# Two GEMM layers of a mixture of experts on one core: the gates' broadcast load and half a layer-two product are moved in the instruction order

## The chip, the cores and the metric

The kernel runs on one core of a Trainium2 chip. The metric is device time in microseconds (us): the median of three executions, 2082.51 us (2081.88 to 2083.3).

## The reference, cut to what matters

Attention and a first MoE come first; the change touches the second MoE alone:

```python
# x: 2304 tokens x 512; w1: 8 experts x 512 x 1024; w2: 8 x 1024 x 512; P: gates, 2304 x 8
P = np.exp(logits - logits.max())
for _ in range(8):
    P /= P.sum(1, keepdims=True) + 1e-09
    P /= P.sum(0, keepdims=True) + 1e-09
    P *= N / E
for e in range(E):
    h = np.maximum(x @ w1[e], 0.0)      # layer one
    out += P[:, e:e+1] * (h @ w2[e])    # layer two
```

## The kernel before, in words

The second MoE runs over three blocks of 768 tokens, and in each block over 16 *quads*, two per expert; a quad m is 512 of an expert's 1024 hidden columns. m counts on over the blocks: m = 0 to 15 is block 0 (its own code, which also prepares the weights and writes them to DRAM), 16 to 31 block 1, 32 to 47 block 2.

Layer one of a quad is 14 products (two 2x2 block multiplications of seven products each, as `GP` lists them). Layer two is 14 half products (seven, as `YP` lists them, each for two halves of the output columns). Float32 is kept by splitting each operand into a high and a low part, so every product or half product is six TensorE matmuls of 384 columns. Layer one's results `rb` (PSUM) are joined and rectified by VectorE and ScalarE into tiles `R`; each `R` is multiplied with the gates (`scaled`, line 1476), and sums and high/low splits of it (lines 1481 to 1500) are layer two's operands `rb`, `rt`. Layer two's results `y` are added to accumulators `a` by VectorE (line 1536).

`scaled` needs the gates of one expert and one token block on all 128 partitions: tile `pb`, 128 x 768 floats, filled by `load_pb` (line 1461) with one DMA that reads six rows of 128 floats for every partition. One `pb` serves two quads, and there are two buffers. Weights come by DMA too: `load_w1` (line 818) brings one layer-one operand `w1o` (256 KB), always the one that is used eight products after the product that has just been written down, into the buffer that this product freed (eight buffers). `w2_op` (line 1512) brings one layer-two operand `w2o` (512 KB; used by two half products) for the next quad; there are nine buffers. Every DMA of this part is issued by SP, in the order in which the code stands, on one queue.

The engines run their instructions in the order in which this code is written; nothing reorders them. Two kinds of code write it:

- `step(m, s)`, 14 steps a quad, for the quads at the ends of a block: m = 16, 17, 31, 32, 33, 47. A step has product s of quad m and then half product s of quad m - 1. In m = 16 there is no such half; steps 0 to 5 hold the last `values` of block 0 instead, whose sums go to `out` by DMA (line 1317), and after step 6 the memory pool of block 0 is closed and its space is given to the tiles of the later blocks, `w2o` among them.
- `run_quad(m)` for quads 18 to 30 and 34 to 46 (`in_runs`): first a *product run*, the quad's 14 products one after the other (in the order `RUN_STEPS`; 14 in that list stands for product 0 of the next quad), then a *layer-two run*, the 14 half products of quad m - 1. The first quad of such a stretch (18, 34) is the *entry*, the last one (30, 46) *leaves*: its product run has no product of the next quad, so only 13 products in that list.

`load_pb` for the next expert stands in every odd quad: in `step` at s == 4, in `run_quad` after product 4 of the product run. The `w2_op` of a quad stand at odd steps; in `run_quad` they are in the layer-two run.

Of the kernel before, what the change touches and what calls it, by code (L numbers as in the profile page):

```python
# [25 lines left out]
def raw(ap):  # L26

    return ap.bitcast(F32)
# [3 lines left out]
def attention_moe_moe2(  # L32
# [40 lines left out]
    NQ = NP // 2  # L73
    PER = NPF // 2
    STEPS = 14
# [50 lines left out]
    def mm3(ps, lhs, rhs, first, last, **kw):  # L126
        (lh, ll), (rh, rl) = lhs, rhs
        nc.tensor.matmul(ps, lhsT=lh, rhs=rh, start=first, stop=False, **kw)  # L128
        nc.tensor.matmul(ps, lhsT=lh, rhs=rl, start=False, stop=False, **kw)  # L129
        nc.tensor.matmul(ps, lhsT=ll, rhs=rh, start=False, stop=last, **kw)  # L130
# [581 lines left out]
    Y_RUN = [YP[i] for i in (0, 1, 4, 2, 5, 3, 6)]  # L712
# [77 lines left out]
    def in_runs(m):  # L790

        return NQ <= m < NB * NQ - 1 and 2 <= m % NQ < NQ - 1
# [398 lines left out]
    def g_product(n, p):  # L1191
        o, b, bk = GP[p]
        first = p in (0, 1, 3)
        if first:
            gb[bk] = g_bank(f"g{bk}") if n else y_bank(f"g{bk}")
        w, x = slab[n][:, o] if n < NP else w1q.pop(7 * n + p), xop[b]
        for k in range(2):
            mm3(
                gb[bk][:, :HALF], (w[:, k, 0], w[:, k, 1]), (x[:, 0, k], x[:, 1, k]), first and k == 0, k == 1,
                skip_group_check=True,  # L1200
            )
# [254 lines left out]
    def load_pb(blk, e):  # L1456

        pbs[blk, e] = pp.tile([P, 2 * HALF], F32, name="pb", tag="pb", bufs=2)
        nt = 2 * HALF // P
        src = d_p.rearrange("(t e) p -> e t p", e=E)[e, blk * nt : (blk + 1) * nt]  # L1460
        nc.sync.dma_start(
            pbs[blk, e].rearrange("p (t c) -> p t c", t=nt), src.unsqueeze(0).to_broadcast([P, nt, P])
        )
# [3 lines left out]
    total = NB * NQ  # L1467
# [4 lines left out]
    def scaled(m, f, h):  # L1472

        pb = pbs[m // NQ, m % NQ // PER][:, h * HALF : (h + 1) * HALF]
        r = R[m, f, h]
        nc.vector.tensor_mul(r, r, pb[:, None, :].to_broadcast([P, 2, HALF]))  # L1476

    def r_sum(m, nm):
        r = {(f, h): R[m, f, h] for f in range(2) for h in range(2)}
        if nm == "t1":  # L1480
            nc.vector.tensor_sub(r[0, 0], r[0, 1], r[0, 0])  # L1481
        elif nm == "t2":
            nc.vector.tensor_sub(r[0, 0], r[1, 1], r[0, 0])
        elif nm == "t3":
            nc.vector.tensor_sub(r[0, 1], r[1, 1], r[0, 1])
        elif nm == "t4":
            nc.vector.tensor_sub(r[1, 0], r[1, 0], r[0, 0])
# [14 lines left out]
    def r_op(m, nm):  # L1502
        r_hi(m, nm)
        if (m, nm) != (total - 1, "b21"):
            r_lo(m, nm, nc.gpsimd)

    def w2_op(m, i):
        if m in PLAIN and i > 3:
            return
        o = (0, 2, 1, 3)[i] if m in PLAIN else (Y_RUN if in_runs(m + 1) else YP)[i][1]  # L1510
        w = w2q[m, o] = wp.tile([P, 2, 2, 2 * P], F32R, name="w2o", tag="w2o", bufs=9)
        nc.sync.dma_start(raw(w), d_w2[m % NQ][:, o])

    def y_product(m, s, order=None):

        i, dt = divmod(s, 2)
        b, op, bk, first, *dsts = (order or (YP_LAST if m in PLAIN else YP))[i]
        if m < total - 1:
            bk %= 2
        ps = yb[2 * bk + dt]  # L1520
        w, x = w2q[m, op], rop[m, b]
        ws = slice(dt * P, (dt + 1) * P)
        for a in range(2):
            mm3(
                ps[:, :HALF], (w[:, a, 0, ws], w[:, a, 1, ws]), (x[:, 0, a], x[:, 1, a]), first and a == 0, a == 1,
                skip_group_check=True,
            )
        for dst in dsts:
            key = (m, dst, dt)
            if m % NQ == 0 and key not in touched:  # L1530
                touched.add(key)
                if dt == 0:
                    acc[dst] = wp.tile([P, 2, HALF], F32, name=f"a{dst[0]}{dst[1]}", tag=f"a{dst[0]}{dst[1]}", bufs=1)
                nc.scalar.copy(acc[dst][:, dt], ps[:, :HALF])
            else:
                nc.vector.tensor_add(acc[dst][:, dt], ps[:, :HALF], acc[dst][:, dt])  # L1536
# [34 lines left out]
    def last_quad():  # L1571
# [23 lines left out]
    OWN_RUN = {  # L1595
        0: ("*10",), 1: ("b11",), 2: ("*01",), 4: ("b21",), 6: ("+t1",), 8: ("t1", "+t3"), 10: ("t3",),
        12: ("b22", "+t2"),
    }
    rbank = []

    def run_ops(m, ops):
        for o in ops:
            if o[0] == "*":
                scaled(m, int(o[1]), int(o[2]))
            elif o[0] == "+":
                r_sum(m, o[1:])
            else:
                r_op(m, o)
# [43 lines left out]
    def run_quad(m):  # L1652

        entry, leave = not in_runs(m - 1), not in_runs(m + 1)
        if entry:
            rfirst[0] = 2 * (m - NQ)
            a = [ps_at.tile([P, 512], F32, name=f"rb{i}", tag="at") for i in range(3)]
            rbank[:] = [a[1], a[0], ps_mm.tile([P, 512], F32, name="rb3", tag="mm"), a[2]]
            run_product(m, 0)
        for s in RUN_STEPS:  # L1660
            if s < 14 or not leave:
                run_product(m, s)
            run_ops(m - 1, (ENTRY_RUN if entry else LATE_RUN).get(s, ()))
            run_ops(m, SCALE_RUN.get(s, ()))
            if s == 4 and m % PER == PER - 1:
                load_pb((m + 1) // NQ, (m + 1) % NQ // PER)
        for s in range(STEPS):
            y_product(m - 1, s, Y_RUN)
            run_ops(m, OWN_RUN.get(s, ()))
            if s % 2:  # L1670
                w2_op(m, s // 2)
        if leave:
            gcount[0] = 3

    def step(m, s):

        nonlocal wp
        if m < total:
            pair, p = divmod(s, 7)

            def rectify(src, f, h):
                if pair == 0:
                    R[m, f, h] = (p3 if m % 2 else p2).tile(
                        [P, 2, HALF], F32, name=f"R{f}{h}", tag="Rb" if m % 2 else "Ra", bufs=4
                    )
                nc.scalar.activation(R[m, f, h][:, pair], src, AF.Relu)  # L1686

            g_product(2 * m + pair, p)
            load_w1(w1_at[14 * m + s] + 8)
        old = NQ <= m - 1 < total  # L1690
        left = in_runs(m - 1)
        if s in EARLY_OPS and m < total:
            scaled(m, *EARLY_OPS[s][1:])
        elif s in LATE_OPS and old and m < total and not (left and s < 4):
            if s == 0:
                scaled(m - 1, 0, 1)
            if m - 1 not in PLAIN:
                r_sum(m - 1, LATE_OPS[s])
        if m < total:
            g_evict(p, rectify)  # L1700
        if s in EARLY_OPS and m < total:
            r_op(m, EARLY_OPS[s][0])
        elif s in LATE_SPLITS and old and m < total and not (left and s < 4):
            if m - 1 not in PLAIN:
                r_op(m - 1, LATE_SPLITS[s])
            elif s == 2:
                r_op(m - 1, "t3")
        if old:
            if m - 1 not in PLAIN:
                y_product(m - 1, s)  # L1710
            else:
                for x in (s,) if s < 12 else (2 * s - 12, 2 * s - 11):
                    y_product(m - 1, x)
        if m < total:
            x_switch(m, s)
            if m > NQ:
                if s % 2:
                    w2_op(m, s // 2)
            elif s < 6:
                values(before, (s,))  # L1720
            elif s == 6:
                wps.close()
                wp = ctx.enter_context(tc.tile_pool(name="wpb", bufs=1))
            elif s % 2:
                for i in range(4) if s == 7 else (s // 2,):
                    w2_op(m, i)
            if s == 4 and m % PER == PER - 1 and m + 1 < total:
                load_pb((m + 1) // NQ, (m + 1) % NQ // PER)
        for d in range(2):
            blk, q = divmod(m - d, NQ)  # L1730
            if q == 0 and blk > 1:
                for dst, at in WHOLE:
                    for x in range(2):
                        if at + x == s + 14 * d:
                            turn_out(blk - 1, dst, x, yb[x] if dst == (1, 0) else None)
# [44 lines left out]
```

## Time and profile before

| | us |
|---|---|
| median of three runs | 2082.51 |
| the profiled execution's own time | 2081.69 |
| its span in the profile | 2080.0 |
| TensorE busy | 2014.5 (97%) |
| VectorE / ScalarE / GpSimd busy | 1433.0 / 911.7 / 1059.1 |

Around the profiled span lie 1.7 us. In the rows below, PE is TensorE, PEld its weight loads, DVE VectorE, ACT ScalarE, POOL GpSimd, SP SyncE; SPq is a DMA issue by SP. A line number is that of the kernel. The stretch that the change touches runs from about 1080 us (m = 16) to the end.

### The profile page before, as it was taken

The numbers are of one execution on the slowest core, as the hardware profiler recorded it, in microseconds if no ns is written. First come the engines' busy times: TensorE is split into PE (matmuls) and PEld (weight loads), VectorE is DVE, ScalarE is ACT, GpSimd is POOL, SyncE is SP. The second block draws the span as 40 slices with busy tenths as digits, with TensorE's granted clock in tenths as the row PEclk, the third lists the DMA queues.
The fourth block names the chain that finished last, engine by engine and source line by source line (L and its number), as shares of the span: only waits on it lengthen the run. The fifth ranks groups of instructions, "written<-read, shape, count | busy, mean of one in ns | idle before, by whom it ended". The sixth has DMA issues, their size and how long they took to land.

```text
span 2080.0 us, 31581 instructions
## 1 busy us (share of the span) xinstructions
PE 2014.5 (97%) x10821; PEld 1836.8 (88%) x10821; DVE 1433.0 (69%) x2572; ACT 911.7 (44%) x1850; POOL 1059.1 (51%) x821
## 2 busy tenths in 40 slices
PE   7989999999999999999999999999999999999999
PEld 5767778777888899999989999999999999999998
DVE  7986776465467887777785667666775666766774
ACT  7766765454354444444444333233234333233322
POOL 4224344341278788887874445444444444444541
PEclk9999999999999999999999999999999999999999
DMA  7877777348478778878889877877787777787773
GB/s 212 275 223 232 229 217 200 110 152 299 154 266 304 303 293 334 319 294 303 314 305 328 253 233 246 266 239 247 252 270 226 252 242 247 249 267 236 242 259 101
DMA packets 296416, 519.68 MB, mean 250 GB/s; under 512 B 91056, under 2 KB 137792, under 8 KB 292160
## 3 DMA queue, kind: packets, MB, share of 16 engines
q1 hardware_dynamic: 296256, 517.65, 74.4%
q8 instruction: 87, 1.43, 0.3%
q14 instruction: 73, 0.60, 0.1%
HBM read 356.53 MB, written 161.03 MB: 249 GB/s over the span
## 4 chain that ended last, share of the span: by engine, by line
PE 76%; DMA 7%; DVE 7%; ACT 3%; issue 1%; POOL 1%; SPq 0%; ACTq 0%; DVEq 0%; POOLq 0%
PE y L129 11%; PE y L130 11%; PE y L128 11%; DMA w1o<-d_w 5%; PE rb L128 5%; PE rb L130 5%; PE rb L129 5%; PE g L128 4%; PE g L130 4%; PE g L129 4%; PE s L128 2%; PE s L129 2%; PE s L130 2%; PE acc L129 2%; PE acc L130 2%; PE acc L128 1%
## 5 line engine op out<-in xcount | busy, mean ns | idle before, releaser
L1500 POOL TENSOR_TENSOR rt<-R,rt 128x768 fp32r<-128x768 f32 x121 | 225.3, 1873 | 255.2 <-ACT rt L1495 237.7
L1500 POOL TENSOR_TENSOR rb<-R,rb 128x768 fp32r<-128x768 f32 x95 | 209.8, 2209 | 266.2 <-ACT rb L1495 256.8
L1536 DVE TENSOR_TENSOR a<-y,a 128x384 f32<-128x384 f32 x420 | 218.3, 549 | 48.9 <-PE y L130 46.0
L1634 DVE CUSTOM_DVE_ANT_0 R<-rb,u 128x384 f32<-128x384 f32 x104 | 58.0, 557 | 221.8 <-ACT u L1643 135.2
L120 POOL TENSOR_TENSOR w2a<-r,w2a 128x1024 fp32r<-128x1024 f32 x64 | 154.0, 2407 | 67.6 <-ACT w2a L119 67.6
L1495 ACT ACTIVATE rt<-R 128x768 fp32r<-128x768 f32 x122 | 100.4, 843 | 193.1 <-DVE R L1481 108.7
L128 PE MATMUL rb<-xt,w1o 128*128 128x384 f32 x416 | 141.0, 339 | 27.0 <-DMA w1o<-d_w 21.4
L128 PE MATMUL y<-rt,w2o 128*128 128x384 f32 x496 | 166.5, 336 | 0.0
L129 PE MATMUL y<-rt,w2o 128*128 128x384 f32 x496 | 166.2, 335 | 0.0
L130 PE MATMUL y<-rt,w2o 128*128 128x384 f32 x496 | 166.2, 335 | 0.0
L1476 DVE TENSOR_TENSOR R<-R,pb 128x768 f32<-128x768 f32 x128 | 160.3, 1253 | 3.0 <-ACT R L1686 2.6
L130 PE MATMUL y<-w2a,rl 128*128 128x512 f32 x384 | 150.2, 391 | 0.0
L129 PE MATMUL y<-w2a,rh 128*128 128x512 f32 x384 | 149.8, 390 | 0.2 <-POOL w2a L120 0.2
L128 PE MATMUL y<-w2a,rh 128*128 128x512 f32 x384 | 149.6, 390 | 0.0
L129 PE MATMUL rb<-xt,w1o 128*128 128x384 f32 x416 | 139.5, 335 | 0.0
L130 PE MATMUL rb<-xt,w1o 128*128 128x384 f32 x416 | 139.4, 335 | 0.0
L128 PE MATMUL y<-rb,w2o 128*128 128x384 f32 x408 | 138.1, 339 | 0.6 <-DVE a L1536 0.6
L129 PE MATMUL y<-rb,w2o 128*128 128x384 f32 x408 | 137.9, 338 | 0.0
L130 PE MATMUL y<-rb,w2o 128*128 128x384 f32 x408 | 137.7, 337 | 0.0
L1495 ACT ACTIVATE rb<-R 128x768 fp32r<-128x768 f32 x96 | 80.8, 842 | 111.8 <-PE y L130 105.5
L1344 ACT ACTIVATE rh<-g 128x384 fp32r<-128x384 f32 x127 | 62.3, 491 | 136.3 <-DVE g L1216 53.5
L1345 DVE SCALAR_TENSOR_TENSOR rl<-g,rh 128x384 fp32r<-128x384 f32 x127 | 70.7, 557 | 69.9 <-ACT rh L1344 69.8
(349 smaller groups left out, 6040.7 us busy)
## 6 DMA issues: line engine op xcount, KB each, us to landing
w1o<-d_w SPq DMA_DIRECT2D x448, 256.0 KB, 3.5
w2o<-d_w SPq DMA_DIRECT2D x218, 512.0 KB, 5.3
d_w<-w1a SPq DMA_DIRECT2D x32, 1792.0 KB, 11.6
d_w<-w2a SPq DMA_DIRECT2D x30, 1536.0 KB, 7.9
r<-in_moe_w_dram SPq DMA_DIRECT2D x64, 512.0 KB, 4.3
u<-in_moe_w_in_dram SPq DMA_DIRECT2D x16, 512.0 KB, 5.0
u<-in_moe_w_out_dram SPq DMA_DIRECT2D x16, 512.0 KB, 5.6
d_in<-a SPq DMA_DIRECT2D x16, 512.0 KB, 2.7
```

Source lines behind the costliest of these rows:

```text
L120: (eng or nc.gpsimd).tensor_sub(lo, src, raw(hi))
L128: nc.tensor.matmul(ps, lhsT=lh, rhs=rh, start=first, stop=False, **kw)
L129: nc.tensor.matmul(ps, lhsT=lh, rhs=rl, start=False, stop=False, **kw)
L130: nc.tensor.matmul(ps, lhsT=ll, rhs=rh, start=False, stop=last, **kw)
L1344: nc.scalar.activation(rh, src, AF.Relu)
L1345: nc.vector.scalar_tensor_tensor(rl, src, 0.0, raw(rh), op0=ALU.max, op1=ALU.subtract)
L1476: nc.vector.tensor_mul(r, r, pb[:, None, :].to_broadcast([P, 2, HALF]))
L1495: nc.scalar.activation(x[:, 0], R[m, f, h], AF.Copy)
L1500: eng.tensor_sub(x[:, 1], R[m, f, h], raw(x[:, 0]))
L1536: nc.vector.tensor_add(acc[dst][:, dt], ps[:, :HALF], acc[dst][:, dt])
L1634: nc.vector._custom_dve(TENSOR_ADD_SAT, out=own(f, h), in0=a, in1=temps[nm], s0=F32_LARGEST, s1=0.0)
```

## The change

There are four edits. (1) In `run_quad`, `load_pb` moves from the product run (after product 4) to the layer-two run (after half product 0). (2) At the entries the `pb` of the entry's expert is loaded one quad sooner: in `step` of m = 16 and 32 in place of m = 17 and 33. (3) The last two `w2o` of the quad ahead of an entry (operands 5 and 6 of m = 17 and 33) are no longer loaded in its steps 11 and 13, but at the start of the entry's layer-two run. (4) In the quads that leave (30, 46), half product 0 of quad m - 1 moves from the head of the layer-two run into the product run, behind product 11. No instruction is added or taken away.

```diff
@@ run_quad
                 run_product(m, s)
             run_ops(m - 1, (ENTRY_RUN if entry else LATE_RUN).get(s, ()))
             run_ops(m, SCALE_RUN.get(s, ()))
-            if s == 4 and m % PER == PER - 1:
+            if leave and s == 11:
+                y_product(m - 1, 0, Y_RUN)
+        for s in range(STEPS):
+            if s or not leave:
+                y_product(m - 1, s, Y_RUN)
+            run_ops(m, OWN_RUN.get(s, ()))
+            if s == 0 and m % PER == PER - 1:
                 load_pb((m + 1) // NQ, (m + 1) % NQ // PER)
-        for s in range(STEPS):
-            y_product(m - 1, s, Y_RUN)
-            run_ops(m, OWN_RUN.get(s, ()))
+            if entry and s < 2:
+                w2_op(m - 1, 5 + s)
             if s % 2:
                 w2_op(m, s // 2)
@@ step
             if m > NQ:
-                if s % 2:
+                if s % 2 and not (in_runs(m + 1) and s > 9):
                     w2_op(m, s // 2)
...
-            if s == 4 and m % PER == PER - 1 and m + 1 < total:
-                load_pb((m + 1) // NQ, (m + 1) % NQ // PER)
+            soon = m + (in_runs(m + 2) and not in_runs(m + 1))
+            if s == 4 and soon % PER == PER - 1 and soon + 1 < total and not in_runs(m + 1):
+                load_pb((soon + 1) // NQ, (soon + 1) % NQ // PER)
```

What this does to the order is shown at three places. SP, quads 18 to 19, before: the layer-two run's seven `w2o` of quad 18, then the product run of quad 19 up to its layer-two run (`d_w_288` and so on are the DRAM tensors of the weights).

```order
L1512 DMA w2o<-d_w_315 128x1024 x7
L818 DMA w1o<-d_w_288 128x512 x3
L818 DMA w1o<-d_w_289 128x512
L1461 DMA pb<-d_p 128x6x128
L818 DMA w1o<-d_w_288 128x512 x2
L818 DMA w1o<-d_w_289 128x512 x4
L818 DMA w1o<-d_w_290 128x512
L818 DMA w1o<-d_w_289 128x512 x2
L818 DMA w1o<-d_w_290 128x512
L1512 DMA w2o<-d_w_316 128x1024 x7
```

The same place on SP after the change:

```order
L1512 DMA w2o<-d_w_315 128x1024 x7
L818 DMA w1o<-d_w_288 128x512 x3
L818 DMA w1o<-d_w_289 128x512
L818 DMA w1o<-d_w_288 128x512 x2
L818 DMA w1o<-d_w_289 128x512 x4
L818 DMA w1o<-d_w_290 128x512
L818 DMA w1o<-d_w_289 128x512 x2
L818 DMA w1o<-d_w_290 128x512
L1461 DMA pb<-d_p 128x6x128
L1512 DMA w2o<-d_w_316 128x1024 x7
```

`pb` moved from between the `w1o` of the product run to the head of the seven `w2o` of the layer-two run.

SP in quad 16, from the `w1o` of step 3 to step 9, before (`out_dram<-o` are the sums of block 0 on their way out):

```order
L818 DMA w1o<-d_w_282 128x512
L1317 DMA out_dram<-o_6842 128x512
L818 DMA w1o<-d_w_282 128x512
L1317 DMA out_dram<-o_6842 128x512
L818 DMA w1o<-d_w_283 128x512 x2
L1512 DMA w2o<-d_w_313 128x1024 x4
L818 DMA w1o<-d_w_283 128x512 x2
L1512 DMA w2o<-d_w_313 128x1024
```

The same place on SP after the change:

```order
L818 DMA w1o<-d_w_282 128x512
L1317 DMA out_dram<-o_6842 128x512
L1461 DMA pb<-d_p 128x6x128
L818 DMA w1o<-d_w_282 128x512
L1317 DMA out_dram<-o_6842 128x512
L818 DMA w1o<-d_w_283 128x512 x2
L1512 DMA w2o<-d_w_313 128x1024 x4
L818 DMA w1o<-d_w_283 128x512 x2
L1512 DMA w2o<-d_w_313 128x1024
```

A `pb` now stands ahead of the last `out` of block 0 and of the first four `w2o`.

TensorE in quad 30, at the end of its product run, before (`xt3`, `xt4`: inputs of products 11 and 12; `rb2`: the PSUM bank that both write):

```order
L129 MATMUL rb2_11931<-xt3_11360,w1o_15315 128x384
L130 MATMUL rb2_11931<-xt3_11360,w1o_15315 128x384
L128 MATMUL rb2_11931<-xt4_11388,w1o_15323 128x384
L129 MATMUL rb2_11931<-xt4_11388,w1o_15323 128x384
L130 MATMUL rb2_11931<-xt4_11388,w1o_15323 128x384
```

The same place on TensorE after the change:

```order
L129 MATMUL rb2_11927<-xt3_11360,w1o_15315 128x384
L130 MATMUL rb2_11927<-xt3_11360,w1o_15315 128x384
L128 MATMUL y0_11534<-rb11_15172,w2o_15175 128x384
L129 MATMUL y0_11534<-rb11_15172,w2o_15175 128x384
L130 MATMUL y0_11534<-rb11_15172,w2o_15175 128x384
L128 MATMUL y0_11534<-rb11_15172,w2o_15175 128x384
L129 MATMUL y0_11534<-rb11_15172,w2o_15175 128x384
L130 MATMUL y0_11534<-rb11_15172,w2o_15175 128x384
L128 MATMUL rb2_11927<-xt4_11388,w1o_15323 128x384
L129 MATMUL rb2_11927<-xt4_11388,w1o_15323 128x384
L130 MATMUL rb2_11927<-xt4_11388,w1o_15323 128x384
```

Six matmuls of layer two came between products 11 and 12, which write the same PSUM bank.

## Rows read from the trace of the kernel before

**Rows 1.** The page: span, then the busy times of the engines.
```profile
span 2080.0 us, 31581 instructions
PE 2014.5 (97%) x10821; PEld 1836.8 (88%) x10821; DVE 1433.0 (69%) x2572; ACT 911.7 (44%) x1850; POOL 1059.1 (51%) x821
```

**Rows 2.** Waits of PE, 1160:1500, then 1660:1995: total, times, longest.
```profile
PE rb L128 <- DMA w1o<-d_w: 10.9, 6, 2.5
...
PE rb L128 <- DMA w1o<-d_w: 10.5, 6, 2.1
```

**Rows 3.** The chain that ended last, 1060:2080: start us, us, what.
```profile
1174.37 9.63 DMA w1o<-d_w
1184.14 0.41 PE rb L128
```

**Rows 4.** Timeline of SP, 1172:1186: start us, us issuing, what.
```profile
1173.74 0.39 SPq L1461 DMA_DIRECT2D pb<-d_p  x1
```

**Rows 5.** DMA issues, 1173.2:1173.4, 1173.7:1173.8, 1174.3:1174.4, 1201:1213: KB each, median us to landing.
```profile
w1o<-d_w SPq DMA_DIRECT2D x1, 256.0 KB, 3.7
...
pb<-d_p SPq DMA_DIRECT2D x1, 384.0 KB, 9.6
...
w1o<-d_w SPq DMA_DIRECT2D x1, 256.0 KB, 9.6
...
w1o<-d_w SPq DMA_DIRECT2D x11, 256.0 KB, 3.1
```

**Rows 6.** Windows (a quiet product run, two stretches, a last product run): busy, clock, DMA, GB/s.
```profile
core 0: us, PE busy (x) PEld busy (x) DVE busy (x) ACT busy (x) POOL busy (x), PEclk, DMA share, GB/s
1200.91:1215.50 14.59, 14.59 (x86) 14.59 (x86) 6.62 (x9) 5.33 (x10) 7.11 (x4) 1.00 0.69 204
1168.95:1503.87 334.92, 324.01 (x1850) 322.28 (x1850) 227.56 (x309) 103.99 (x165) 154.92 (x78) 0.99 0.78 249
1662.17:1996.63 334.46, 323.98 (x1849) 322.24 (x1849) 227.55 (x309) 104.00 (x165) 154.90 (x78) 0.99 0.77 249
1503.87:1518.26 14.39, 13.82 (x79) 13.50 (x79) 6.62 (x9) 4.85 (x9) 7.12 (x4) 1.00 0.68 201
```

**Rows 7.** Windows at a low clock behind a wait, and at quad 16's end.
```profile
1306.25:1309.60 3.35, 3.35 (x12) 3.35 (x11) 1.42 (x2) 0.46 (x1) 0.00 (x0) 0.50 0.84 263
...
1100.00:1112.00 12.00, 10.63 (x60) 10.01 (x59) 9.11 (x9) 6.41 (x12) 6.69 (x4) 1.00 0.94 352
```

**Rows 8.** Timeline of SP, 1186.6:1204: a layer-two run's loads.
```profile
1186.89 10.37 SPq L1512 DMA_DIRECT2D w2o<-d_w  x7
1202.17 1.36 SPq L818 DMA_DIRECT2D w1o<-d_w  x2
```

**Rows 9.** The chain that ended last, 1096:1112, in quads 16 and 17.
```profile
1096.23 3.57 DMA out_dram<-o
...
1099.81 0.02 SPq L1512
...
1101.83 7.66 DMA w1o<-d_w
...
1109.62 0.41 PE g L128
```

**Rows 10.** Timeline of SP, 1114.7:1117, then DMA issues, 1115.4:1115.6 and 1116.6:1116.8.
```profile
1115.48 0.32 SPq L818 DMA_DIRECT2D w1o<-d_w  x1
1116.71 0.37 SPq L1461 DMA_DIRECT2D pb<-d_p  x1
...
w1o<-d_w SPq DMA_DIRECT2D x1, 256.0 KB, 7.2
...
pb<-d_p SPq DMA_DIRECT2D x1, 384.0 KB, 10.7
```

**Rows 11.** Waits of PE, 1500:1520 (a last product run), then 1120:1150 (an entry).
```profile
PE rb L128 <- ACT u L1643: 0.6, 1, 0.6
...
PE rb L128 <- ACT u L1641: 1.9, 1, 1.9
```

## The prediction

> **What bounds the kernel now.** I read the page first: TensorE is busy 2014.5 of 2080.0 us, the next engine 1433.0 [rows 1]. So a gain has to come out of TensorE's 65 idle us or out of stretches at a low clock; work moved on other engines counts only if TensorE waits for it. Next come TensorE's waits in the two stretches of run quads (19 to 29, and 35 to 45): nothing is listed there but `w1o`, six waits each, 10.9 and 10.5 us together [rows 2]. The chain of waits shows what such a wait is: a `w1o` takes 9.63 us to land and TensorE starts again 0.14 us after it [rows 3]; there are twelve such pairs, one in every odd quad. The timeline of SP shows what stands ahead of it: `pb`, issued at 1173.74 [rows 4]. By the list of DMA issues the `w1o` just ahead of this `pb` lands in 3.7 us, `pb` itself in 9.6 and the `w1o` just behind it in 9.6; in the product run of an even quad, without `pb`, it is 3.1 [rows 5]. A `w1o` is issued eight products ahead. A product run of 14 takes 14.59 us when nothing waits [rows 6], so a product takes 1.04 us and the lead is 8.3 us. 3.1 us fit, 9.6 don't: the reader is to see that TensorE pays for `pb` through the queue, not for the gates, which are read much later.
>
> **Edit 1, `pb` into the layer-two run: -27.4 us.** The idle time (21.4 us) is not the whole price. I take it from lengths: the two stretches take 334.92 and 334.46 us and hold 22 runs each of 14.59 us, 320.98 us [rows 6]; 13.9 and 13.5 us are lost, 27.4 together. The 6 us above the idle time are the restart (the matmul behind a wait takes 0.41 us [rows 3], where matmuls otherwise follow each other every 0.17) and the low clock: behind two of the twelve waits the granted clock is 0.50, the 1.2 GHz level, for about 3.4 us (one of them in [rows 7]), which costs half of that, 1.7 us, each time. Without the waits both go.
>
> What is late next? The product runs of even quads have the same instructions on all engines and run without a wait in 14.59 us, so no other engine steps in. In its new place `pb` delays the seven `w2o` behind it. They are for the next quad's layer-two run, a whole product run (14.6 us) later; and nothing else follows on SP until the next product run: the seven are issued from 1186.89 within 10.4 us, the next `w1o` at 1202.17 [rows 8]. The queue's work in that time: seven `w2o` of 512 KB at the best rate seen, 352 GB/s [rows 7], 1.49 us each, 10.4 us; `pb` about 4.7 us (below) to at most 6.3; 15.1 to 16.7 us, against some 15 us until the first `w1o`. At most 1.7 us stay over, and a `w1o` has 8.3 - 3.1 = 5.2 us to spare. Price: 0.
>
> **Edit 4, half a layer-two product in the last product runs: -1.7 us.** Products 11 and 12 write one bank; TensorE waits 0.6 us for ScalarE to copy it [rows 11]. By length: 13 products should take 13 x 1.04 = 13.55 us and take 14.39 [rows 6], 0.84 us lost, twice. Six matmuls (1.04 us) between them cover the wait; their own time was spent in the layer-two run before and is only moved. VectorE's addition for them comes ahead of two other short ones; it is busy 6.62 of 14.39 us there [rows 6]. If the cover failed, it would cost these 1.7 us back and no more.
>
> **Edit 2, the entry's `pb` a quad sooner: +4.7 us.** This is where the change costs. In quad 16 TensorE already waits on the queue: the chain goes from the last `out` of block 0 (landed at 1099.80) over SP, which held the first four `w2o` until then because they take over that memory, to a `w1o` that lands 7.66 us after its issue, and TensorE starts at 1109.62 [rows 9]. The DMA engines are 0.94 busy at 352 GB/s [rows 7]. The `pb` now stands ahead of that last `out`, so everything on this chain comes later by `pb`'s own time in the queue, and TensorE with it. Of that time: 1115.48 + 7.2 = 1122.7 is the landing of the `w1o` ahead of quad 17's `pb`, 1116.71 + 10.7 = 1127.4 that of the `pb`: 4.7 us [rows 10]. In the run the same difference is 6.3 (1173.3 + 3.7 to 1173.74 + 9.6 [rows 4, 5]), with less queued ahead of it to cover its start. The queue in quad 16 is the fuller one, so I take 4.7; the bounds are 0 (if the queue had room that the DMA share hides) and 6.3, and one stretch at the low clock, 1.7 us, on top. What quad 17 no longer has to load gives nothing back: TensorE's only wait from 1120 to 1150 is one for ScalarE, at the entry [rows 11]. In block 2 (quad 32) no memory is handed over, and a step is two products long, so the lead is 16.7 us; price 0.
>
> The Trainium skill, "DMA: Bandwidth & Descriptors", section Specifications, states that transfers of at least 512 B run at line rate. `pb` is made of pieces of 128 floats, 512 B, so by that rule it would pass as fast per byte as the weights; the trace does not agree, since it has 4.7 us for 384 KB of `pb` [rows 10], and the sum goes by the measurement.
>
> **Edit 3, two `w2o` of the entry: 0.** They are issued at the head of the entry's layer-two run and first read at its half product 10, 10 x 1.04 = 10.4 us later; nothing but `w1o` that land in 3.1 us [rows 5] is queued ahead, and each `w2o` adds its 1.49 us: 4.6 and 6.1 us. Only with a `pb` ahead of them (at most 6.3 more) would the first be late, by 0.5 us; none stands there in quads 18 and 34.
>
> **Sum.** -27.4 - 1.7 + 4.7 = -24.4 us. Against the profiled execution, 2081.7, that is 2057.3; this one lies 0.8 below the median of the runs, 2082.5, so the forecast is 2058.
>
> **Rivals.** (a) The entry costs more: the waits that 4.7 us make in quads 16 and 17 bring the low clock once or twice, or `pb` takes the 6.3 us: +1.7 to +5, 2060 to 2063. For it: two of the twelve waits were followed by the clock at 0.50; against it: ten were not. (b) The entry is nearly free: `pb` passes quad 16's queue at the best rate seen, 352 GB/s [rows 7], which is 1.1 us for 384 KB in place of 4.7, and the time is 2054 to 2055 (2053 if nothing is left of it). Against it speak the differences of 4.7 and 6.3 us. The rule of the skill quoted at edit 2 would bring this case. (c) `pb` comes through in the layer-two run and half of the twelve waits return in the next product run, +14, 2072. (d) Slower: in the layer-two run the queue does not speed up to 352 GB/s but stays at the 204 GB/s of a quiet run [rows 6]. Then seven `w2o` take 18.0 us and `pb` 4.7, 22.7 us against 15, and 7.7 us stay over; that is 2.5 us more than the 5.2 to spare, in each of twelve odd quads: +30, 2088. It decides from an overhang of 5.2 us, and makes the kernel slower from one of 7.2 us, where each of the twelve waits costs the 2.0 us that the whole gain of 24.4 comes to. Against it: 204 GB/s is what the kernel asks for in that run, not what the queue can give. (e) The waits were not `pb`'s and stay: 2082.5 - 1.7 + 4.7, 2085.5; against it speak the even quads, without `pb` and without a wait.
>
> **How the numbers follow.** Forecast (2055 to 2060) 0.55; (a) 0.25; (b) 0.08; (c) 0.06; (d) 0.03; (e) 0.03. The range from 2052 to 2066 holds the forecast, (a) and (b), 0.88, and leaves out (c) to (e). A measurement of this kernel can tell 0.2%, 4.2 us, from no change. Faster by more than that are the forecast and (a) to (c), 0.94; within it most of (e), 0.03; slower (d), 0.03.
>
> **What would show it.** Right: no wait of TensorE for `w1o` between the entries and the leaves; every product run 14.59 us; `w1o` landings of about 3 us in odd quads; the two last product runs without the 0.6 us wait; in quad 16 the `w1o` of the wait at 1109.62 landing 4 to 6 us later, and no new wait in quads 17, 32 and 33. Wrong: waits for `w1o` or `w2o` in odd quads' layer-two runs or behind them, or a shift at quad 16 far from 4.7 us.

## The result and the profile after

The changed kernel takes 2059.26 us (median of four runs, 2059.02 to 2059.86); the kernel before 2082.91 (2081.88 to 2083.37). The ratio is 0.9888 [0.987, 0.9905]: faster by 1.1%. The forecast was 2058, its range 2052 to 2066. The page, as [rows 1]: the span is 22.5 us shorter; the work on VectorE, ScalarE and GpSimd is the same, and TensorE's busy time is 3.6 us less.

```profile
span 2057.5 us, 31576 instructions
PE 2010.9 (98%) x10821; PEld 1836.3 (89%) x10821; DVE 1433.2 (70%) x2572; ACT 911.7 (44%) x1850; POOL 1059.4 (51%) x821
```

Windows of the changed kernel, columns as in [rows 6]: the two stretches of run quads, a last product run (13 products and now the half product), quad 16 from its step 6 to the entry, and two stretches at a low clock.

```profile
1175.66:1496.57 320.91, 320.91 (x1850) 320.91 (x1850) 227.46 (x309) 103.98 (x165) 154.98 (x78) 1.00 0.79 259
1654.13:1975.03 320.90, 320.90 (x1849) 320.90 (x1849) 227.45 (x309) 103.98 (x165) 154.96 (x78) 1.00 0.78 257
1496.57:1511.20 14.63, 14.63 (x85) 14.63 (x85) 7.17 (x10) 4.85 (x9) 7.11 (x4) 1.00 0.80 250
1097.58:1142.24 44.66, 40.53 (x217) 40.21 (x216) 21.53 (x28) 19.87 (x38) 17.23 (x9) 0.92 0.85 299
17.80:24.40 6.60, 6.21 (x26) 5.56 (x27) 2.97 (x9) 4.64 (x14) 3.44 (x7) 0.50 0.98 286
1106.50:1113.40 6.90, 5.27 (x16) 5.27 (x17) 3.24 (x4) 3.39 (x7) 3.47 (x2) 0.51 0.86 321
```

The same windows of the kernel before, where no row stands ahead of the prediction: quad 16 from step 6 to the entry, and the start.

```profile
1095.25:1135.03 39.78, 38.41 (x218) 37.78 (x217) 21.83 (x28) 20.11 (x38) 17.72 (x9) 1.00 0.93 345
17.80:24.40 6.60, 5.99 (x31) 5.03 (x31) 4.14 (x13) 5.13 (x17) 3.35 (x6) 0.74 0.99 296
```

The two stretches are now what 22 quiet runs take, 320.9 us, with TensorE busy throughout: 14.0 and 13.6 us less than in [rows 6]. Without the half product's 1.04 us the last product run is 13.59, against 14.39. Quad 16 costs 4.9 us more. These and 0.5 us at the entry of quad 18, which in the profile of before fell into a low clock, sum to -27.6 - 1.6 + 4.9 - 0.5 = -24.8 us from step 6 of quad 16 to the end. The spans differ by 22.5 only, because step 6 begins 2.3 us later (1097.58 for 1095.25): the first 130 us held more of the low clock, the window 17.80:24.40 first of all. None of the four edits reaches there, and the last experiment shows that it isn't the change's. Quads 31 to 33, the other place where an entry's `pb` now comes a quad sooner (quad 32), take 95.96 us (from 1524.75) for 95.91 (from 1532.85), so it costs nothing there.

In the new place `pb` does delay what is behind it, and nothing there is late. SP's timeline in quad 19's layer-two run (start us, us issuing), then DMA issues in that run and in the product run after it (KB each, median us to landing), then the landing of all the `pb` from 1160 to 1965:

```profile
1190.87 0.37 SPq L1461 DMA_DIRECT2D pb<-d_p  x1
1191.30 9.89 SPq L1512 DMA_DIRECT2D w2o<-d_w  x7
```

```profile
w2o<-d_w SPq DMA_DIRECT2D x7, 512.0 KB, 10.3
...
w1o<-d_w SPq DMA_DIRECT2D x11, 256.0 KB, 3.2
...
DMA to landing us min/median/max: 8.2/8.9/9.8
```

`pb` itself is as slow as before (9.6 in [rows 5]). The `w1o` of the next product run land in a median of 3.2 us, close to the 3.1 of [rows 5], but the first of them are slower. This is the one that lands closest to its use, in the product run behind another `pb`: its issue, its landing, and TensorE's first matmul with it:

```profile
1859.60 2.40 SPq L818 DMA_DIRECT2D w1o<-d_w  x3
...
w1o<-d_w SPq DMA_DIRECT2D x1, 256.0 KB, 5.3
...
1866.69 0.33 PE L128 MATMUL rb<-xt,w1o 128*128 128x384 f32 x1
```

It lands at 1864.9, 1.8 us ahead of its use. So the seven `w2o` and `pb` do reach into the next product run, by some 2 us, and the lead of the `w1o` covers it.

Quad 16 has the size that was forecast, but TensorE waits for another engine than was foreseen. Its waits from 1090 to 1160 (total, times, longest), where before it waited for a `w1o` at 1109.62 [rows 9]:

```profile
PE g L128 <- ACT u L1214: 4.1, 1, 4.1
PE rb L128 <- ACT u L1641: 2.6, 2, 1.9
```

It waits for ScalarE, which copies a PSUM bank that product 12 needs. ScalarE's timeline shows why that copy is late (in brackets: idle us ahead, and what the trace names as its end):

```profile
1106.87 0.84 ACT L1495 ACTIVATE rb<-R 128x768 fp32r<-128x768 f32 x1 [4.38 <-DMA w1o<-d_w]
1107.62 0.46 ACT L1214 COPY u<-g 128x384 f32<-128x384 f32 x1
```

The copy at 1107.62 stands behind a high/low split (line 1495), and ScalarE sat 4.38 us ahead of this split. It writes the first `rb` in memory that came from block 0. In the kernel before, the same split had no such wait:

```profile
1100.83 0.85 ACT L1495 ACTIVATE rb<-R 128x768 fp32r<-128x768 f32 x1 [0.68 <-DVE R L1476]
```

SP's timeline of the same microseconds in the changed kernel, the landing of the `out` issued at 1098.56, and SP's own wait for it:

```profile
1096.14 0.34 SPq L1317 DMA_DIRECT2D out_dram<-o  x1
1096.53 0.43 SPq L1461 DMA_DIRECT2D pb<-d_p  x1
1097.07 0.57 SPq L818 DMA_DIRECT2D w1o<-d_w  x1
1098.56 0.34 SPq L1317 DMA_DIRECT2D out_dram<-o  x1
1099.33 1.61 SPq L818 DMA_DIRECT2D w1o<-d_w  x2
1106.68 0.32 SPq L1512 DMA_DIRECT2D w2o<-d_w  x1
...
out_dram<-o SPq DMA_DIRECT2D x1, 256.0 KB, 8.0
...
SPq L1512 <- DMA out_dram<-o: 5.6, 1, 5.6
```

The last `out` is behind `pb` and lands at 1098.56 + 8.0 = 1106.6 (before: 1099.80 [rows 9]). SP's first `w2o` goes out at 1106.68 and the split starts at 1106.87; the split waits on several DMAs, and the name `w1o` beside it is only the one that the trace puts last. By these times one landing stops two engines. SP's stop was foreseen; ScalarE's reaches TensorE first. In the 4.1 us wait (1104.0 to 1108.1) the granted clock falls, and from 1106.5 it is 0.51, the 1.2 GHz level, for 6.9 us.

The path that was foreseen is there all the same, behind that. This is the first `w1o` behind the four `w2o`, the one that TensorE waited for at 1109.62 before: its issue, its landing, and TensorE's first matmul with it:

```profile
1108.52 0.99 SPq L818 DMA_DIRECT2D w1o<-d_w  x2
...
w1o<-d_w SPq DMA_DIRECT2D x1, 256.0 KB, 7.6
...
1116.92 0.34 PE L128 MATMUL g<-xt,w1o 128*128 128x384 f32 x1
```

It lands at 1116.1. Counted from step 6 that is 18.5 us, where it was 14.2 (1109.48, [rows 9]): 4.3 us later, within the 4 to 6 us that the prediction asked for. TensorE gets there 0.8 us after it, 5.0 us later than before, because ScalarE and the low clock had held it longer. The two paths run side by side from one landing, and the longer one hides the other.

### The profile page after: what moved, and what is told of

It is laid out like the page before. It is cut to its first block, busy times and chain, and to the rows that moved or that the text cites. A ratio compares the mean times of both kernels' runs of the same rounds, so it can differ in the third digit from the quotient of the medians.

```text
span 2057.5 us, 31576 instructions
## 1 busy us (share of the span) xinstructions
PE 2010.9 (98%) x10821; PEld 1836.3 (89%) x10821; DVE 1433.2 (70%) x2572; ACT 911.7 (44%) x1850; POOL 1059.4 (51%) x821
## 4 chain that ended last, share of the span: by engine, by line
PE 81%; DVE 6%; ACT 2%; DMA 2%; issue 1%; POOL 1%; SPq 0%; ACTq 0%; DVEq 0%; POOLq 0%
PE y L129 11%; PE y L130 11%; PE y L128 11%; PE rb L128 6%; PE rb L130 6%; PE rb L129 6%; PE g L128 4%; PE g L130 4%; PE g L129 4%; PE s L128 2%; PE acc L129 2%; PE acc L130 2%; PE s L130 2%; PE s L129 2%; PE acc L128 2%
```

## The experiments

Each was timed beside the kernel before. The intervals are 0.13 to 0.25% (3 to 5 us) to either side, so smaller differences are read from stretch lengths in the profiles (us):

| kernel | step 6 of quad 16 begins | step 6 to entry | entry to end | step 6 to end |
|---|---|---|---|---|
| before | 1095.25 | 39.78 | 944.9 | 984.7 |
| changed | 1097.58 | 44.66 | 915.3 | 960.0 |
| entry's `pb` back | 1094.99 | 40.21 | 916.1 | 956.3 |
| leaving half back | 1095.27 | 45.04 | 917.3 | 962.4 |
| two `w2o` back | 1096.84 | 43.86 | 915.3 | 959.1 |
| `pb` in product run | 1097.64 | 44.29 | 942.3 | 986.6 |
| `pb` behind last `out` | 1096.79 | 43.12 | 915.8 | 959.0 |
| more gate rows | 1096.58 | 44.18 | 994.0 | 1038.2 |
| before, gates by expert | 1095.88 | 39.98 | 917.4 | 957.4 |
| changed, gates by expert | 1095.37 | 39.59 | 916.0 | 955.6 |
| entry back, gates by expert | 1096.99 | 38.98 | 916.4 | 955.4 |
| changed, again | 1094.84 | 44.75 | 915.3 | 960.0 |

**Edit 2 undone.**

```diff
-            soon = m + (in_runs(m + 2) and not in_runs(m + 1))
-            if s == 4 and soon % PER == PER - 1 and soon + 1 < total and not in_runs(m + 1):
-                load_pb((soon + 1) // NQ, (soon + 1) % NQ // PER)
+            if s == 4 and m % PER == PER - 1 and m + 1 < total:
+                load_pb((m + 1) // NQ, (m + 1) % NQ // PER)
```

> The changed kernel with edit 2 alone undone: the entry's pb is loaded in quads 17 and 33 again. Theory (pb in quad 16 stands ahead of the last out of block 0, and what waits for that out's landing, ScalarE's first split into the taken-over memory and SP's first w2o, comes about 5 us later): 2054.3 us, 5 less than the changed kernel; TensorE's 4.13 us wait in quad 16 becomes the 0.57 and 0.80 us waits of the kernel before, no 6.8 us at the low clock there, and quads 17 and 33 show no new wait. Rival (pb in quad 17 has lost its cover, because edit 3 moved two w2o and the run that follows now has no slack): a wait for w1o in quad 17 or 18, 2059 or more. Rival (the 4.13 us wait is ScalarE's own and not pb's): 2059, wait unchanged.

Measured: 2053.12 us, ratio 0.9857 [0.984, 0.9873]. Waits of TensorE from 1095 to 1160, and the window from step 6 to the entry:

```profile
PE rb L128 <- ACT u L1641: 1.9, 1, 1.9
PE g L128 <- DMA w1o<-d_w: 1.3, 1, 1.3
PE g L128 <- ACT u L1214: 0.6, 1, 0.6
...
1094.99:1135.20 40.21, 38.39 (x218) 37.77 (x216) 21.91 (x28) 20.10 (x38) 17.74 (x9) 1.00 0.93 330
```

The 4.1 us wait and the low clock that came with it are gone, and no new wait came in quad 17. This edit costs 4.4 us there. From the entry on, the changed kernel is 0.8 us ahead (915.3 for 916.1), all of it at quad 18's entry, where this profile, like that of before, has 3.4 us at a granted clock of 0.50 and the changed one has none. So the edit costs 3.7 us in all, and without it the kernel is faster than the changed one.

**Edit 4 undone.**

```diff
-            if leave and s == 11:
-                y_product(m - 1, 0, Y_RUN)
...
-            if s or not leave:
-                y_product(m - 1, s, Y_RUN)
+            y_product(m - 1, s, Y_RUN)
```

> The changed kernel with edit 4 alone undone: half product 0 stands at the head of the layer-two run again in quads 30 and 46. Theory (TensorE waits there for ScalarE to copy the bank that products 11 and 12 share, 0.84 us by the length of the run): two waits of 0.57 us come back, +1.7 us, 2061.0. Rival (the half product only moved the wait to another place, or the gain of it was in what followed): 2059.3, with the waits back or another one gone.

Measured: 2059.92 us, ratio 0.989 [0.9873, 0.9906]. The wait of [rows 11] is back. Product run and layer-two run of a leaving quad together take 28.98 us for 28.18, 0.80 each and 1.6 in both: what edit 4 is worth, though the times alone couldn't tell it from nothing.

**Edit 3 undone.**

```diff
-            if entry and s < 2:
-                w2_op(m - 1, 5 + s)
...
-                if s % 2 and not (in_runs(m + 1) and s > 9):
+                if s % 2:
```

> The changed kernel with edit 3 alone undone: the two w2o of the quad ahead of an entry are loaded in its steps 11 and 13 again. Theory (edit 3 is worth nothing once pb is out of quad 17): 2059.3, within 0.5, no wait for w1o in quads 17, 18, 33, 34. Rival (it relieves the queue at the entry, whose w1o would be late without it): +1 to +2 us, with a wait for w1o in quad 18, more than in 34 because quad 16's queue is longer.

Measured: 2057.41 us, ratio 0.9878 [0.9862, 0.9895]. No wait for `w1o` or `w2o` came, the entry to the end is the same 915.3, and the 0.8 us in quad 16 go with a low clock of 3.4 us there in place of 6.8 (in all the profiles with this wait, 6.8 us go with 44.7 to 45.0 us from step 6 to the entry, 3.4 us with 43.9 to 44.3). Edit 3 is worth nothing either way.

**Edit 1 undone**, all else as changed.

```diff
+            if s == 4 and m % PER == PER - 1:
+                load_pb((m + 1) // NQ, (m + 1) % NQ // PER)
             if leave and s == 11:
...
-            if s == 0 and m % PER == PER - 1:
-                load_pb((m + 1) // NQ, (m + 1) % NQ // PER)
```

> The changed kernel with edit 1 alone undone: pb behind product 4 of the odd quads' product runs again; the entry's pb, the two w2o and the half product stay as changed. Theory (the twelve waits for w1o are pb's place in the queue, 27.4 us): 2059.3 + 27.4, 2086.7, slower than the kernel before by the entry's price less 1.7; twelve waits of 1.4 to 2.5 us for w1o. Rival (part of the gain of the runs is that of edits 2 to 4): under 2080.

Measured: 2086.19 us (12 runs), ratio 1.0014 [1.0001, 1.0028]. Waits of TensorE from 1160 to 1520 and from 1660 to 2000:

```profile
PE rb L128 <- DMA w1o<-d_w: 10.4, 6, 2.2
...
PE rb L128 <- DMA w1o<-d_w: 9.8, 6, 2.1
```

All twelve waits are back, and from entry to end the kernel takes 27.0 us more than the changed one (942.3 for 915.3). Edit 1 is the whole gain; the other three together cost about 2 us from step 6 on (986.6 for 984.7).

**The queue or the stops?** The entry's `pb` is issued two steps later: behind the last `out` and the two `w1o` beside it, ahead of one more `w1o` and the first four `w2o`.

```diff
-            if s == 4 and soon % PER == PER - 1 and soon + 1 < total and not in_runs(m + 1):
+            if s == (6 if m == NQ else 4) and soon % PER == PER - 1 and soon + 1 < total and not in_runs(m + 1):
```

> The changed kernel, but quad 16's pb is issued two steps later (step 6): behind the last out of block 0 and still ahead of the first four w2o. Theory of the prediction (what counts is pb's time in the queue, about 4.9 us, for everything issued behind it: the w2o and w1o that TensorE needs next): ScalarE's 4.4 us stop for the out's landing is gone, TensorE waits for w2o and w1o instead, and the time from quad 16's step 6 to quad 18 stays near 44.7 us; total 2059. Rival (what costs is that ScalarE is stopped by the out's landing; the weights behind pb would still be in time): that time falls to the 39.9 us of the kernel before, total 2054.

Measured: 2057.48 us, ratio 0.9867 [0.9849, 0.9885]. Waits of TensorE from 1095 to 1142, of ScalarE from 1101 to 1104, of SP from 1096 to 1104, and the window from step 6 to the entry:

```profile
PE y L128 <- DMA w2o<-d_w: 2.8, 1, 2.8
PE g L128 <- DMA w1o<-d_w: 1.1, 1, 1.1
PE g L128 <- ACT u L1214: 0.6, 1, 0.6
...
ACT rb L1495 <- DMA w1o<-d_w: 0.7, 1, 0.7
...
SPq L1512 <- DMA out_dram<-o: 2.2, 1, 2.2
...
1096.79:1139.91 43.12, 38.61 (x217) 37.70 (x216) 23.30 (x28) 20.18 (x38) 17.44 (x9) 1.00 0.87 316
```

ScalarE's stop shrinks from 4.38 to 0.7 us, SP's from 5.6 to 2.2, and the low clock goes, yet TensorE now waits 2.8 us for a `w2o`. So without either stop, `pb` in the queue still costs 43.1 - 39.8 = 3.3 us, between the two expectations. This does not divide the 4.9 us between SP and ScalarE: both stops went together, and two `w1o` changed places with `pb`. No run takes away ScalarE's stop alone. That the split waits for the `out`'s landing fits here too: the first `w2o` is issued at 1102.25, the split starts at 1102.40.

**How much fits into the layer-two run?** Behind each `pb` there, 8 more rows of 128 gates are read for every partition, into idle `o` buffers that nobody reads.

```diff
+    def more_pb(blk, e, times):
+        nt = 2 * HALF // P
+        src = d_p.rearrange("(t e) p -> e t p", e=E)[e, blk * nt : blk * nt + 4]
+        for _ in range(times):
+            x = wp.tile([P, 2, 2 * P], F32, name="o", tag="o", bufs=2)
+            nc.sync.dma_start(x.rearrange("p a (b c) -> p (a b) c", c=P), src.unsqueeze(0).to_broadcast([P, 4, P]))
...
                 load_pb((m + 1) // NQ, (m + 1) % NQ // PER)
+                more_pb((m + 1) // NQ, (m + 1) % NQ // PER, 2)
```

> The changed kernel with eight more rows of 128 gates read by every partition right behind each pb of a layer-two run (two loads of four rows into buffers that lie idle there; their contents are not used): 14 rows in place of 6 stand ahead of the seven w2o. Theory (the layer-two run has room for one pb in the queue because a w1o has 5.2 us to spare, not without limit): at 0.8 to 1.0 us a row the overhang at the end of the run grows from about 1 to 6.4 to 10 us, and each of the twelve odd quads waits 1.2 to 5 us for w1o at the start of the next product run: 2073 to 2119 us. Rival (order alone matters: in the layer-two run such loads disturb nobody): 2059, no wait for w1o.

Measured: 2138.5 us, ratio 1.0254 [1.0229, 1.0278]. Waits of TensorE from 1160 to 2070, then SP's timeline in quads 18 and 19, the DMA issue from 1206 to 1207, and a window behind the first wait:

```profile
PE rb L128 <- DMA w1o<-d_w: 55.4, 12, 5.7
...
1189.37 0.37 SPq L1461 DMA_DIRECT2D pb<-d_p  x1
1189.80 1.08 SPq L1471 DMA_DIRECT2D o<-d_p  x2
1190.93 14.66 SPq L1522 DMA_DIRECT2D w2o<-d_w  x7
1206.50 9.29 SPq L818 DMA_DIRECT2D w1o<-d_w  x8
...
w1o<-d_w SPq DMA_DIRECT2D x1, 256.0 KB, 9.6
...
1213.80:1220.60 6.80, 4.41 (x14) 4.44 (x15) 0.00 (x0) 0.48 (x1) 0.94 (x1) 0.50 0.92 326
```

With 14 rows in place of 6 the seven `w2o` need 14.66 us to be issued (9.89 in the changed kernel), the first `w1o` of the next product run lands in 9.6, and TensorE waits in every one of the twelve product runs behind a `pb`, 4.6 us on the mean, each time with a stretch of 3.4 or 6.8 us at the low clock that reaches beyond the wait. So the mechanism of rival (d), an overhang longer than the lead, is real, and the limit lies between 6 and 14 rows. The time lies above the 2073 to 2119 us expected: the waits are within the 1.2 to 5 us on the mean, but from entry to end they cost 994.0 - 915.3 = 78.7 us, 6.6 each, and the expectation had left out the low clock.

**Is it the place of `pb` or its cost?** The kernel before, none of the four edits, but the gates are laid out by expert in DRAM: `pb` then reads one piece of 3 KB for a partition instead of six of 512 B. The bytes are the same.

```diff
-        nc.scalar.copy(lg, pe)
+        nc.scalar.copy(rows.rearrange("p (e t) -> p t e", e=E), pe)
...
-        src = d_p.rearrange("(t e) p -> e t p", e=E)[e, blk * nt : (blk + 1) * nt]
-        nc.sync.dma_start(
-            pbs[blk, e].rearrange("p (t c) -> p t c", t=nt), src.unsqueeze(0).to_broadcast([P, nt, P])
-        )
+        src = d_p.rearrange("(e t) p -> e (t p)", e=E)[e, blk * nt * P : (blk + 1) * nt * P]
+        nc.sync.dma_start(pbs[blk, e], src.unsqueeze(0).to_broadcast([P, nt * P]))
```

> The kernel before, nothing moved, but the gates are stored in DRAM expert by expert, so that pb reads one piece of 3 KB for every partition instead of six of 512 B; same bytes, a sixth of the pieces. Theory (pb's 4.7 to 6.5 us in the queue come from its 768 small pieces): about 1.1 us at 352 GB/s, a w1o behind it lands in about 4.3 us of its 8.3, the twelve waits go and with them 27.4 us: 2055. Rival (they come from the bytes, or from 128 partitions reading the same DRAM rows): pb as before, twelve waits, 2083.

Measured: 2055.36 us, ratio 0.9859 [0.9838, 0.988]. No wait of TensorE is listed in the stretches. DMA issues of a `pb` and the `w1o` behind it, the landing of all the `pb` from 1160 to 1960, that of the kernel before with six pieces (1160 to 2000), and the first stretch:

```profile
pb<-d_p SPq DMA_DIRECT2D x1, 384.0 KB, 6.0
...
w1o<-d_w SPq DMA_DIRECT2D x1, 256.0 KB, 5.8
...
DMA to landing us min/median/max: 4.2/5.0/6.0
...
DMA to landing us min/median/max: 8.3/8.7/9.6
...
1169.27:1490.18 320.91, 320.91 (x1850) 320.91 (x1850) 227.45 (x309) 104.13 (x165) 155.01 (x78) 1.00 0.79 260
```

The `w1o` behind `pb` still comes later than the usual 3.1 us and than the 4.3 expected, but 5.8 is within the lead, and the stretch is 320.91 us, as in the changed kernel. The waits came from what `pb` takes of the queue; to move it elsewhere is one answer, to make it cheap another. The new layout has fewer pieces, and they also lie side by side in DRAM, where the six were 4 KB apart; which of the two makes `pb` cheap was not separated.

**Both together**: the changed kernel, and the changed kernel without edit 2, with the same two edits of the layout.

> The changed kernel with the gates stored expert by expert in the same way. Theory (the entry costs what pb takes in the queue): quad 16's price falls from 4.9 to about 1.1 us, ScalarE's wait for the last out from 4.4 to under 1 us; 2055. Rival (the price is that of one more load ahead of the out, whatever its pieces): 2059.

> Edits 1, 3 and 4 with the entry's pb back in quads 17 and 33, and the gates stored expert by expert: the version that the runs so far point to. Theory (pb's place in the queue matters no longer once it is 128 pieces): nothing left to win over the same without the new layout or over the changed kernel with it, 2053 to 2055; from quad 16's step 6 to the end 955 to 957 us. Rival (the two savings add up): under 2052.

Measured: 2054.68 us, ratio 0.9854 [0.9836, 0.9873], and 2054.47 us, ratio 0.9855 [0.9841, 0.987]. Step 6 to the entry of the first:

```profile
1095.37:1134.96 39.59, 38.38 (x217) 37.76 (x216) 21.92 (x28) 20.11 (x38) 17.74 (x9) 1.00 0.88 324
```

With a cheap `pb` the entry's early load costs nothing (39.59 for 39.78; 1.1 us was expected): it takes `pb`'s price and its place together to make the 4.9 us of quad 16. The savings don't add, since both remove the same twelve waits: 955 to 957 us from step 6 on, however it is done. The four versions at 2053 to 2055 beat both kernels, and these runs don't tell them from each other.

**The changed kernel once more**, for the 2.3 us ahead of step 6.

> The changed kernel once more, beside the version above on one chip. Theory: 4 to 5 us above it, all of it between quad 16's step 6 and quad 18 (44 to 45 us there, 40 in the version above); the first step 6 of quad 16 begins between 1095 and 1098 us whatever the kernel, by how long the clock is low in the first 130 us. Rival (the change itself made the part before quad 16 longer by 2.3 us): 1097.6 us again, while the other kernels begin at 1095 to 1096.

Measured: 2058.08 us, ratio 0.9876 [0.986, 0.9893]. Step 6 begins at 1094.84, and from there to the end it takes the same 960.0 us; its granted clock in 17.80:24.40 is 0.74, as in the kernel before. The other profiles agree: the five with 10.2 us of low clock between 16 and 130 us begin step 6 at 1096.8 to 1097.6, those with 3.4 us at 1094.8 to 1095.9. The 2.3 us were the low clock at the start of one execution.

## Why the prediction was right, point by point

- The sum, forecast -24.4: measured -24.7 from step 6 of quad 16 to the end. The profiled execution came out 1.3 us above 2058 all the same, because 2.3 us of low clock at its start are in it, which no term of the sum is about.
- Edit 1, forecast -27.4: measured -27.6 in the two stretches, and 27.0 when it alone is undone. The price read from lengths was right, where the listed idle time (21.4) would have been 6 us short.
- What is late next, forecast nothing: right, but with less room than the prediction had. Its lead of 8.3 us is too long: a `w1o` is issued when its buffer is free, so seven products and not eight lie ahead of its use, and 1859.60 to 1866.69 is 7.1 us. In the kernel before, the `w1o` issued at 1174.37 was the one with the wait of 2.5 us [rows 2, 3], so TensorE was ready at 1181.6, 7.3 us after the issue. To spare are then 7.1 - 3.1 = 4.0 us, not 5.2, and at most 5.3 - 3.1 = 2.2 of them are used, near the forecast's overhang of at most 1.7. With 14 rows of gates in place of 6 they don't suffice.
- Edit 4, forecast -1.7: measured -1.6. Edit 3, forecast 0: measured 0.
- Edit 2, forecast +4.7: measured +4.9 in quad 16 of the changed kernel, and 4.4 there when undone. The step "everything on this chain comes later by `pb`'s own time in the queue, and TensorE with it" holds for the chain that it names, SP, `w2o` and a late `w1o`: that `w1o` came 4.3 us later. But TensorE was stopped before that by ScalarE, whose split waited for the same `out`, and reached the `w1o`'s product 5.0 us later. The row that would have warned is the split itself, which in the profile of before begins at 1100.83, 1 us after the last `out` has landed. Both paths hang on one landing, so it is not by chance that both are some 4 us long; but the prediction had not worked out the one that decided, nor its low clock, and that this came to only 0.7 us more is luck. In quads 32 and 33, forecast 0: measured 0.
- Rivals: (a)'s low clock came, 6.9 us of it, inside the 4.9 us rather than on top; (b) is what the cheap `pb` does, not this one; (c) and (e) are excluded by the stretches without a wait, and (d) by them and by the queue's speed: it moves 364 GB/s from 1198 to 1206, in the layer-two run of quad 19, not 204.

## What to carry to other kernels

A load in a shared queue is priced by what lands behind it, and by the lead of that, counted from the issue to the first use: the twelve waits belonged to `pb`, though each was a wait for a `w1o`. Before moving such a load, ask first whether fewer, longer pieces make it cheap where it is; and list everything that waits for the landing of the transfers that it is moved past, buffers handed over between pools among them, on every engine and not on the issuing one alone. A price read from the length of a stretch holds the restart and the clock; the sum of idle times does not.

## What the runs showed of the hardware

- The same 384 KB, at the same place in the order, land in a median of 8.7 us as six 512 B pieces for each partition and in 5.0 as one piece of 3 KB (kernel before, and with the gates by expert).
- A granted clock of 0.50 came in stretches of some 3.4 or 6.8 us. One began during or just behind two of the twelve waits of 1.4 to 2.5 us in the kernel before, all twelve waits of 3.4 to 5.7 us with more gate rows, the 4.1 us wait of the changed kernel in both of its profiles, and the 1.9 us wait at quad 18's entry in the kernel before, but not in the changed one.
- In this program, ScalarE's first write into memory taken over from a closed pool began only after a transfer out of that pool had landed: 4.4 us of ScalarE for one 256 KB `out`.
